# Fewer load buffers for the attention stage of an attention and mixture-of-experts kernel

## The chip, the cores and the metric

The kernel runs on one core of a Trainium2 chip. The metric is the device time of one execution in microseconds (us). The engines of the core are TensorE (PE), VectorE (DVE), ScalarE (ACT), GpSimd (POOL) and SyncE (SP); all loads and stores spoken of here are transfers that SP starts and that the core's 16 DMA engines carry out.

## What is computed

Attention over 4 batches and 8 heads, 768 tokens, head dimension 64, all in float32: each query sees the keys less than 16 tokens away and 24 summaries, one for each block of 32 tokens (the elementwise maximum of the block's keys, the mean of its values). Its output, laid out as tokens by 512, feeds a mixture of 8 experts with one expert per token, where a token may keep the expert of the token before it.

```python
k_sum = k.reshape(B, H, nb, block, D).max(axis=3)      # block 32, nb 24
v_sum = v.reshape(B, H, nb, block, D).mean(axis=3)
scores_l = scale * q @ k^T, masked to |i - j| < 16
scores_s = scale * q @ k_sum^T + log(block)
a = softmax(concat([scores_l, scores_s], axis=-1))
x = a @ concat([v, v_sum])                             # (B, S, H * D)
...
for s in range(S):                                     # for each batch b
    e = argmax(logits[b, s]) if s == 0 or local_gate[b, s] < 0.5 else prev_e
    out[b, s] = p[e] * (relu(x[b, s] @ w1[e]) @ w2[e])
```

## The kernel before

Attention works on 16 pairs of heads (4 batches of 4 pairs, `N = len(pairs)`), each pair `n` in two groups `G = 2n` and `2n + 1` of half the tokens. Four loads feed a pair: its keys into a `kp` buffer (`load_k`, 384 KB), its queries into `q` (`load_q`, 384 KB), its values into `vt` (`load_v`, 384 KB), and the values again, arranged as windows, into `vw` (`load_w`, 768 KB). K, Q, V and W below mean these four. Buffers are taken in turn, so pair `n` uses buffer `n % NK` and so on; a load into a buffer waits for the last reader of the pair that had it before.

The readers are these. Of `kp`: the block maxima on DVE (`reduce_k`, L245) and the copies into windowed keys `kb` on POOL (`windows`, L277), both one group or so before the pair's own scores. Of `q`: the score matmuls `s_mm` (L370) of both groups. Of `vt`: POOL's fold, DVE's sum and the gate matmuls (`gate_v`) in the pair's second group. Of `vw`: the output matmuls `a_mm` (L405), which come three groups after the scores (`LA = 3`); beside the loaded part of `vw`, POOL's `spread_v` (L307) and ACT's `gate_t` write the block means and gates into it. One group runs through `s_mm` on PE into `bs`, its maxima on DVE (`s_max`, L376, `nm`), the exponentials on ACT, transposes on PE, `a_mm` into `ba`, and the normalization on DVE into `xs`. Between these, the loop weaves in routing work for the tokens already done (L827, L858).

The order is written out by hand: `opening(G)` for the first six groups, then a loop over `G` in which each group's steps stand in a fixed order and `load_*` is called for a pair a few pairs ahead. Everything that SP does goes through it in program order, and an instruction that waits holds all that stand behind it. Beside the loads SP issues eight stores of finished attention output to DRAM (`x_dram`, 876 KB each, L567, two per batch, some groups after the batch's last pair), two constant loads at the end of `opening(4)`, one register load (`e_93`, L1380) and, when group 27 is through, the fetch of four weight chunks (`wst`, L1096, 512 KB each) of the first expert; four more follow after attention. An early DVE and POOL stretch clears the margins of the `kp`, `vt` and `vw` buffers once.

After attention (from about 118 us to the end) the experts' matmuls run; tokens are gathered from `x_dram` by POOL (L1118), transposed on PE (L1129), and the first weights are cast on ACT (`wcast`, L1373) into memory that the attention's buffers held before.

```python
NQ, NK, NV, NVW, NX = 5, 4, 4, 5, 4
```

Of the kernel before, what the change touches and what calls it, by code (L numbers as in the profile page):

```python
# [80 lines left out]

C_T, C_PE, C_WAIT, C_LONG, C_DVE, C_LAT, AHEAD = 0.65, 0.8, 0.3, 1.3, 0.14, 0.05, 1.5

NQ, NK, NV, NVW, NX = 5, 4, 4, 5, 4

LOCAL_THR = -1.4e-7

# [1 line left out]
class Kernel:  # L89
# [82 lines left out]
    def attention(self, tick, last):  # L172
        nc, tc, ident = self.nc, self.tc, self.ident
        with ExitStack() as ctx:
# [17 lines left out]
            def load_k(n):  # L192
                b, p = pairs[n]
                nc.sync.dma_start(out=kp[n % NK][:, 16:16 + S], in_=self.kT[b, p])

            def load_v(n):
                b, p = pairs[n]
                nc.sync.dma_start(out=vt[n % NV][:, 16:16 + S], in_=self.vT[b, p])

            def load_q(n):  # L200
                b, p = pairs[n]
                nc.sync.dma_start(out=qs[n % NQ], in_=self.qT[b, p])

            def load_w(n):
                b, p = pairs[n]
                nc.sync.dma_start(out=vw[n % NVW][:, AUX:NPL - AUX].rearrange("p j t c -> p (j t c)"), in_=self.vW[b, p][:, 0:P * NW])
# [36 lines left out]
            def reduce_k(n):  # L243
                ks = kss[n] = wk.tile([P, NB], F32, name="ks")
                nc.vector.tensor_reduce(out=ks, in_=by32(kp[n % NK][:, 16:16 + S]), op=ALU.max, axis=AX.X)  # L245
# [37 lines left out]
            def one_row(n):  # L283
                return groups[GATHER + 1][0] <= n
# [64 lines left out]
            def s_mm(G):  # L349

                n, g = groups[G]
                sp = live[G] = self.two_banks()
                quarters = [(h, c) for c in range(2) for h in range(2)]

                def at(h, c):
                    u = sp[64 * c:64 * c + 64, h, 0:NG * W].rearrange("p (u w) -> p u w", u=NG)
                    return slice(64 * h, 64 * h + 64), u

                for h, c in quarters:
                    r, o = at(h, c)
                    m0 = W * (2 * g + c)
                    nc.tensor.matmul(out=o.rearrange("p u w -> p (u w)"), lhsT=eye2[r], rhs=mask2[r, m0:m0 + NG * W],
                                     start=True, stop=False)
                for u in range(NG):
                    for h, c in quarters:
                        r, o = at(h, c)
                        t = 2 * (NG * g + u) + c
                        nc.tensor.matmul(out=o[:, u, :], lhsT=qs[n % NQ][r, 64 * t:64 * t + 64], rhs=kb[n % 2][r, t, :],  # L370
                                         start=False, stop=(u == NG - 1))

            def s_max(G):
                sp = live[G][:, :, 0:NG * W].rearrange("p h (u w) -> p h u w", u=NG)
                nm = wk.tile([P, 2, NG], F32, name="nm")
                nc.vector.tensor_reduce(out=nm, in_=sp, op=ALU.max, axis=AX.X, negate=True)  # L376
                live[G] = sp, nm
# [62 lines left out]
            def opening(G):  # L440

                s_mm(G)
                s_max(G)
                if G == 0:
                    s_exp(0)
                    reduce_k(1)
                    summaries(1)
                    gate_sums(True)
                    loads = (load_v, 2), (load_k, 3), (load_q, 3)
                elif G == 1:  # L450
                    gate_v(0)
                    s_exp(1)
                    reduce_v(0)
                    loads = (load_w, 2), (load_v, 3), (load_k, 4), (load_q, 4)
                elif G == 2:
                    sum_v(0)
                    spread_v(0)
                    s_exp(2)
                    gate_t(0)
                    t_stage(0)  # L460
                    loads = (load_v, 4), (load_w, 3)
                elif G == 3:
                    windows(2, nc.scalar, 0, NW // 2)
                    windows(2, nc.gpsimd, NW // 2, NW)
                    t_stage(1)
                    reduce_v(1)
                    reduce_k(2)
                    summaries(2, nc.vector)
                    gate_v(1)
                    s_exp(3)  # L470
                    a_mm(0)
                    a_norm(0)
                    loads = (load_k, 5), (load_q, 5)
                elif G == 4:
                    sum_v(1)
                    spread_v(1)
                    gate_t(1)
                    s_exp(4)
                    t_stage(2)
                    a_mm(1)  # L480
                    reduce_v(2)
                    reduce_k(3)
                    a_norm(1)
                    windows(3)
                    summaries(3)
                    loads = (load_v, 5), (load_w, 4)
                else:
                    keep = gate_v(2)
                    keep()
                    t_stage(3)  # L490
                    s_exp(5)
                    a_mm(2)
                    a_norm(2)
                    spread_v(2)
                    fold_v(3)
                    loads = (load_k, 6), (load_q, 6)
                for load, n in loads:
                    load(n)
                if G == 4:
                    for t, src in consts:  # L500
                        nc.sync.dma_start(out=t, in_=src)
# [9 lines left out]
            for G in range(OPEN, last_g + LA):  # L511
                tick(G, 6)
                if G == last_g:
                    ctx2.close()
                    self.split_weights()
                    self.free_banks()
                    self.clock()
                if G < last_g:
                    s_mm(G)
                n, g = divmod(G, GP)  # L520
                keep = gate_v(n) if g == 1 and n < len(pairs) else None
                if keep and one_row(n):
                    keep()
                if g == 0 and n <= len(pairs):
                    gate_t(n - 1)
                if LT <= G < last_g + LT:
                    t_stage(G - LT)
                if G < last_g:
                    s_max(G)
                    s_exp(G)  # L530
                    if G == OPEN:
                        reduce_v(3, folded.pop(3))
                    if keep and not one_row(n):
                        keep()
                    self.small(TIME[groups[G][1] if G < MORE else GP][0], True)
                tick(G, 0)
                if G < last_g:
                    self.small(TIME[groups[G][1] if G < MORE else GP][1], True)
                n, g = divmod(G, GP)
                if g == 1 and n < len(pairs) - 1:  # L540
                    reduce_v(n + 1, folded.pop(n + 1))
                if g == 0 and n < len(pairs) - 1:
                    reduce_k(n + 1)
                if LA <= G:
                    a_mm(G - LA)
                    a_norm(G - LA)
                if G < last_g:
                    n, g = groups[G]
                    N = len(pairs)
                    if g == 0:  # L550
                        if n + 1 < N:
                            windows(n + 1)
                            fold_v(n + 1)
                        if n + 2 < N:
                            if n + 3 < N:
                                load_v(n + 3)
                            load_w(n + 2)
                    else:
                        if n + 1 < N:
                            summaries(n + 1)  # L560
                        spread_v(n)
                        if n + 4 < N:
                            load_k(n + 4)
                            load_q(n + 4)
                while stores and stores[0][0] <= G:
                    _, t, x = stores.pop(0)
                    nc.sync.dma_start(out=self.x_dram[:, t:t + NG, :], in_=x.rearrange("p u a d -> p u (a d)"))  # L567
                tick(G, 5)
                tick(G, 1)
                if G < last_g:  # L570
                    self.small(TIME[groups[G][1] if G < MORE else GP][2], True)
                else:
                    self.flow(C_T)
# [1146 lines left out]
```

## Time and profile before

| | us |
|---|---|
| median of 3 runs (lowest, highest) | 414.23 (413.96, 414.83) |
| the profiled execution's own time | 417.37 |
| span of its trace | 415.6 |
| attention in it, to about | 118 |

The profiled execution is one more execution, with the profiler on; its own time stands 3.14 us above the median, and the span, from the first to the last instruction, 1.8 us below its own time. A row of a timeline is a run of like instructions: when the first started, the time to the end of the last, engine, line, operation, output and inputs with their shapes, how many, and in brackets how long the engine had stood idle before it and what ended that; "issue" there means that nothing in the profile was waited for. SPq is SP's queue of DMA issues: its rows tell when transfers were started, not when they landed. A window row tells how long each engine was busy in a stretch and with how many instructions.

### The profile page before, as it was taken

How to read it: one execution, taken by the hardware profiler on the slowest of the kernel's cores; microseconds unless marked ns; L12 is line 12 of the kernel's file. 1: busy time of each engine (PE TensorE's matmuls, PEld its weight loads, DVE VectorE, ACT ScalarE, POOL GpSimd, SP SyncE). 2: the span in 40 equal slices, each digit the busy share in tenths (PEclk: the TensorE clock that was granted, in tenths of full speed). 3: DMA queues.
4: the chain of work that ended last, by engine and by line, in shares of the span. 5: the costliest groups of instructions: out<-in, count | busy, mean ns of one | idle time of the engine just before them, and what ended most of it. 6: DMA issues, size and time to landing. Idle time of an engine off the chain costs nothing. (4 is left out here: it accounts for less than half of the span.)

```text
span 415.6 us, 10447 instructions
## 1 busy us (share of the span) xinstructions
PE 401.2 (97%) x3802; PEld 332.5 (80%) x3802; DVE 232.8 (56%) x516; ACT 186.9 (45%) x461; POOL 199.1 (48%) x334
## 2 busy tenths in 40 slices
PE   7999999999999999999999999999999999999993
PEld 6678777778798888888877877888998888889882
DVE  4778978989687777685232222263537433312631
ACT  4978877788874322156221002251535422101550
POOL 7599877877769300258503310063716460010552
PEclk9999999999999999999999999999999999999998
DMA  8999999999490200857777464128353670010011
GB/s 298 412 410 407 410 401 409 386 377 334 109 353 32 84 26 0 337 224 252 267 275 250 135 222 147 83 53 294 93 186 108 233 223 35 26 53 25 2 49 34
DMA packets 21936, 83.70 MB, mean 201 GB/s; under 512 B 2638, under 2 KB 3152, under 8 KB 18800
## 3 DMA queue, kind: packets, MB, share of 16 engines
q1 hardware_dynamic: 17600, 68.49, 44.2%
q0 software_dynamic: 4128, 14.22, 9.9%
q8 instruction: 32, 0.52, 0.5%
q10 hardware_dynamic: 144, 0.20, 0.2%
q14 instruction: 32, 0.26, 0.2%
HBM read 69.43 MB, written 13.60 MB: 200 GB/s over the span
## 5 line engine op out<-in xcount | busy, mean ns | idle before, releaser
L1253 ACT ACTIVATE hT<-bs 128x256 fp32r<-128x256 f32 (+1 forms) x88 | 34.6, 394 | 116.2 <-PE bs L1292 64.2
L1255 DVE SCALAR_TENSOR_TENSOR hT<-bs,hT 128x256 fp32r<-128x256 f32 (+1 forms) x88 | 38.3, 435 | 72.1 <-ACT hT L1253 72.0
L1147 PE MATMUL ba<-h,hT 128*128 128x512 f32 x192 | 77.9, 406 | 0.0
L1149 PE MATMUL ba<-h,hT 128*128 128x512 f32 x192 | 75.1, 391 | 0.0
L1148 PE MATMUL ba<-l,hT 128*128 128x512 f32 x192 | 74.9, 390 | 0.0
L1171 POOL DMA_INDIRECT out_dram<-yo,sidx x23 | 25.7, 1116 | 77.3 <-DVE yo L1163 36.7
L1290 PE MATMUL bs<-xT,h 128*128 128x512 f32 (+1 forms) x160 | 61.1, 382 | 0.0
L1291 PE MATMUL bs<-xT,h 128*128 128x512 f32 (+1 forms) x160 | 60.6, 379 | 0.0
L1292 PE MATMUL bs<-xT,l 128*128 128x512 f32 (+1 forms) x160 | 60.6, 379 | 0.0
L1118 POOL DMA_INDIRECT xg<-x_dram,gidx x26 | 30.0, 1154 | 62.6 <-PE ba L1149 27.5
L384 ACT ACTIVATE pr<-bs,nm 128x120 f32<-128x120 f32 x192 | 52.1, 382 | 4.8 <-DVE nm L376 4.5
L1109 POOL TENSOR_TENSOR l<-stg,h 128x256 fp32r<-128x256 f32 x48 | 37.6, 814 | 14.9 <-ACT h L1101 14.8
L1149 PEld LDWEIGHTS ba<-h,hT 128*128 128x128 f32 x192 | 36.0, 188 | 7.9
L1147 PEld LDWEIGHTS ba<-h,hT 128*128 128x128 f32 x192 | 36.1, 188 | 7.2 <-issue 0.8
L307 POOL COPY vw<-gs 24x432 f32<-24x432 f32 (+2 forms) x83 | 34.2, 431 | 15.5 <-issue 10.9
L1148 PEld LDWEIGHTS ba<-l,hT 128*128 128x128 f32 x192 | 36.2, 188 | 6.4
L1101 ACT CAST h<-stg 128x1024 fp32r<-128x1024 f32 x32 | 32.5, 1048 | 12.8 <-PE ba L1149 9.9
L1104 DVE TENSOR_TENSOR l<-stg,h 128x1024 fp32r<-128x1024 f32 x20 | 30.3, 1525 | 10.9 <-ACT h L1101 10.6
L1290 PEld LDWEIGHTS bs<-xT,h 128*128 128x128 f32 x160 | 30.0, 188 | 5.4 <-PE bs L1205 0.4
L1291 PEld LDWEIGHTS bs<-xT,h 128*128 128x128 f32 x160 | 30.0, 188 | 5.1 <-DVE xT L1124 0.2
L1292 PEld LDWEIGHTS bs<-xT,l 128*128 128x128 f32 x160 | 30.0, 188 | 5.0
L405 PE MATMUL ba<-vw,pt 121*64 121x76 f32 x768 | 32.5, 233 | 1.2 <-DMA vt<-in_vT 0.7
(271 smaller groups left out, 676.9 us busy)
## 6 DMA issues: line engine op xcount, KB each, us to landing
stg<-in_w SPq DMA_DIRECT2D x16, 1024.0 KB, 5.7
vw<-in_vW SPq DMA_DIRECT2D x16, 768.0 KB, 10.5
raw<-in_w SPq DMA_DIRECT2D x8, 1024.0 KB, 8.2
x_dram<-xs SPq DMA_DIRECT2D x8, 876.0 KB, 9.6
kp<-in_kT SPq DMA_DIRECT2D x16, 384.0 KB, 7.8
q<-in_qT SPq DMA_DIRECT2D x16, 384.0 KB
vt<-in_vT SPq DMA_DIRECT2D x16, 384.0 KB, 9.2
wst<-in_w SPq DMA_DIRECT2D x8, 512.0 KB, 9.2
```

Of the source, the lines that this page charges most:

```text
L307: nc.gpsimd.tensor_copy(out=bass.AP(dst.tensor, dst.offset, [dst.ap[0], (step, planes), (4, NW), (1, m)]), in_=bass.AP(src.tensor, src.off ...
L384: nc.scalar.activation(out=pr[:, h, u, :], in_=sp[:, h, u, :], func=AF.Exp, bias=nm[:, h, u:u + 1], scale=1.0)
L405: nc.tensor.matmul(out=ap[64 * c:64 * c + 64, u, h], lhsT=pt[0:W + 1, h, u, 64 * c:64 * c + 64], rhs=vw[n % NVW][0:W + 1, PL * h:PL * h + ...
L1109: eng.tensor_tensor(out=lo[:, p], in0=src[:, p], in1=hi[:, p].bitcast(F32), op=ALU.subtract)
L1147: nc.tensor.matmul(out=ps, lhsT=ah, rhs=wh, start=first, stop=False)
L1148: nc.tensor.matmul(out=ps, lhsT=ah, rhs=wl, start=False, stop=False)
L1149: nc.tensor.matmul(out=ps, lhsT=al, rhs=wh, start=False, stop=last)
L1253: self.nc.scalar.activation(out=h, in_=ps, func=AF.Relu)
L1255: self.nc.vector.scalar_tensor_tensor(out=l, in0=ps, scalar=0.0, in1=h.bitcast(F32), op0=ALU.max, op1=ALU.subtract)
L1290: nc.tensor.matmul(out=ps, lhsT=wh, rhs=xh[k], start=(k == 0), stop=False)
L1291: nc.tensor.matmul(out=ps, lhsT=wh, rhs=xl[k], start=False, stop=False)
L1292: nc.tensor.matmul(out=ps, lhsT=wl, rhs=xh[k], start=False, stop=(k == KT - 1))
```

## The change

The numbers of buffers go from 5 to 3 for queries, 4 to 2 for keys, 4 to 3 for values and 5 to 3 for value windows; the output buffers (`NX`) stay 4. The loads are asked for correspondingly later, as a buffer must be free: in the loop, the even group of pair `n` asks for W of pair `n + 1` (before: V of `n + 3`, then W of `n + 2`), and the odd group for K, Q and V of pair `n + 3` (before: K and Q of `n + 4`). The lists of `opening` follow suit. Nothing is changed in what is computed.

```diff
-NQ, NK, NV, NVW, NX = 5, 4, 4, 5, 4
+NQ, NK, NV, NVW, NX = 3, 2, 3, 3, 4
...
                 if G == 0:
-                    loads = (load_v, 2), (load_k, 3), (load_q, 3)
+                    loads = (load_v, 2), (load_k, 3)
                 elif G == 1:
-                    loads = (load_w, 2), (load_v, 3), (load_k, 4), (load_q, 4)
+                    loads = (load_q, 3), (load_w, 2), (load_v, 3)
                 elif G == 2:
-                    loads = (load_v, 4), (load_w, 3)
+                    loads = ()
                 elif G == 3:
-                    loads = (load_k, 5), (load_q, 5)
+                    loads = (load_k, 4), (load_q, 4), (load_v, 4)
                 elif G == 4:
-                    loads = (load_v, 5), (load_w, 4)
+                    loads = ((load_w, 3),)
                 else:
-                    loads = (load_k, 6), (load_q, 6)
+                    loads = (load_k, 5), (load_q, 5), (load_v, 5)
...
                         if n + 1 < N:
                             windows(n + 1)
                             fold_v(n + 1)
-                        if n + 2 < N:
-                            if n + 3 < N:
-                                load_v(n + 3)
-                            load_w(n + 2)
+                            load_w(n + 1)
                     else:
                         if n + 1 < N:
                             summaries(n + 1)
                         spread_v(n)
-                        if n + 4 < N:
-                            load_k(n + 4)
-                            load_q(n + 4)
+                        if n + 3 < N:
+                            load_k(n + 3)
+                            load_q(n + 3)
+                            load_v(n + 3)
```

On PE and ACT the instructions stand in the same order as before, but for the numbers of buffers; DVE has four and POOL six clearing instructions fewer at the start. What moves is SP's row. In the rows below, the name after DMA is the buffer with its number (`kp_125<-in_kT` loads keys), and the brackets name the semaphores waited for: DMAHW0 to DMAHW7 count finished transfers, each used by every eighth, and DVE, PE, Pool and Activation count that engine's work. The first place is the steady state on SP, from the keys of pair 12 on, in the kernel before:

```order
L194 DMA kp_125<-in_kT 128x768 [waits DMAHW6_49,DVE_49,Pool_49]
L202 DMA q_122<-in_qT 128x768 [waits DMAHW7_49]
L198 DMA vt_131<-in_vT 128x768 [waits DMAHW0_49,PE_49,Pool_49]
L206 DMA vw_136<-in_vW 128x1536 [waits DMAHW1_49,Activation_49]
L194 DMA kp_126<-in_kT 128x768 [waits DMAHW2_49,DVE_49,Pool_49]
L202 DMA q_123<-in_qT 128x768 [waits DMAHW3_49]
L567 DMA x_dram<-xs_142 128x3x584 [waits DMAHW4_49,DVE_49]
```

The same place on SP in the changed kernel, from the keys of pair 12 up to the second store of the batch:

```order
L194 DMA kp_123<-in_kT 128x768 [waits DMAHW6_49,DVE_49,Pool_49]
L202 DMA q_120<-in_qT 128x768 [waits DMAHW7_49,PE_49]
L198 DMA vt_127<-in_vT 128x768 [waits DMAHW0_49,PE_49]
L565 DMA x_dram<-xs_135 128x3x584 [waits DMAHW1_49]
L206 DMA vw_132<-in_vW 128x1536 [waits DMAHW2_49,PE_49,Activation_49]
L565 DMA x_dram<-xs_136 128x3x584 [waits DMAHW3_49,DVE_49]
```

Q and W now wait for PE too, and the keys and queries of pair 13, which stood ahead of the batch's first store, come after its second (the register load of L1378 stands between). The W in both is that of pair 11. The second place is the end of attention on SP, the last rows of loads, the weights and the third batch's stores, in the kernel before:

```order
L206 DMA vw_139<-in_vW 128x1536 [waits DMAHW7_49,Activation_49]
L206 DMA vw_135<-in_vW 128x1536 [waits PE_49,DMAHW0_49,Activation_49,Pool_49]
L1096 ISA
L1096 DMA wst_2230<-in_w 128x1024 [waits DMAHW1_49]
...
L1096 DMA wst_2236<-in_w 128x1024 [waits DMAHW4_49]
L567 DMA x_dram<-xs_140 128x3x584 [waits DMAHW5_49,DVE_49]
L567 DMA x_dram<-xs_141 128x3x584 [waits DMAHW6_49,DVE_49]
```

The same on SP in the changed kernel:

```order
L206 DMA vw_132<-in_vW 128x1536 [waits DMAHW7_49,PE_49,Activation_49]
L1094 ISA
L1094 DMA wst_2212<-in_w 128x1024 [waits DMAHW0_49]
...
L1094 DMA wst_2218<-in_w 128x1024 [waits DMAHW3_49]
L206 DMA vw_130<-in_vW 128x1536 [waits PE_49,DMAHW4_49,Activation_49,Pool_49]
L565 DMA x_dram<-xs_133 128x3x584 [waits DMAHW5_49,DVE_49]
L565 DMA x_dram<-xs_134 128x3x584 [waits DMAHW6_49,DVE_49]
```

The W of the last pair, which stood ahead of the four weight fetches, now stands behind them and just ahead of the two stores.

## Rows read from the trace of the kernel before

**Rows 1.** Page, busy us of each engine, share of the span, instructions:

```profile
PE 401.2 (97%) x3802; PEld 332.5 (80%) x3802; DVE 232.8 (56%) x516; ACT 186.9 (45%) x461; POOL 199.1 (48%) x334
```

**Rows 2.** Page: packets, MB, share of a queue; issues, KB each, median us to landing:

```profile
q8 instruction: 32, 0.52, 0.5%
...
vw<-in_vW SPq DMA_DIRECT2D x16, 768.0 KB, 10.5
...
x_dram<-xs SPq DMA_DIRECT2D x8, 876.0 KB, 9.6
```

**Rows 3.** Timeline of SP's issues: start us, us, line, output and input, count:

```profile
77.87 0.33 SPq L194 DMA_DIRECT2D kp<-in_kT  x1
...
83.29 5.04 SPq L206 DMA_DIRECT2D vw<-in_vW  x2
88.54 2.36 SPq L1096 DMA_DIRECT2D wst<-in_w  x4
93.55 3.89 SPq L567 DMA_DIRECT2D x_dram<-xs  x2
```

**Rows 4.** Timeline of PE, 48 to 108 us, output matmuls and "issue" stops:

```profile
51.82 1.01 PE L405 MATMUL ba<-vw,pt 121*64 121x76 f32 x24
...
68.26 0.42 PE L370 MATMUL bs<-kb,q 64*64 64x120 f32 x4 [0.93 <-issue]
...
74.89 0.57 PE L370 MATMUL bs<-kb,q 64*64 64x120 f32 x10 [0.20 <-issue]
...
79.77 1.01 PE L405 MATMUL ba<-vw,pt 121*64 121x76 f32 x24
81.62 0.64 PE L370 MATMUL bs<-kb,q 64*64 64x120 f32 x15 [0.27 <-issue]
...
88.80 0.83 PE L370 MATMUL bs<-kb,q 64*64 64x120 f32 x21 [0.48 <-issue]
...
100.72 1.01 PE L405 MATMUL ba<-vw,pt 121*64 121x76 f32 x24
```

**Rows 5.** Timeline of DVE, 60 to 92 us, the instructions after idle time:

```profile
68.73 0.91 DVE L376 TENSOR_REDUCE nm<-bs 128x6 f32<-128x720 f32 x1 [0.66 <-PE bs L370]
69.90 0.23 DVE L332 COPY gs<-bt 64x73 f32<-64x73 f32 x1 [0.26 <-ACT gs L329]
75.49 0.91 DVE L376 TENSOR_REDUCE nm<-bs 128x6 f32<-128x720 f32 x1 [0.16 <-PE bs L370]
76.67 0.23 DVE L332 COPY gs<-bt 64x73 f32<-64x73 f32 x1 [0.27 <-ACT gs L329]
```

**Rows 6.** Windows: us; busy (count) PE, PEld, DVE, ACT, POOL; clock, DMA share, GB/s:

```profile
48.49:54.79 6.30, 5.99 (x126) 4.76 (x126) 5.15 (x10) 4.80 (x17) 5.37 (x12) 1.00 1.03 401
68.23:74.87 6.64, 6.43 (x125) 5.12 (x126) 5.71 (x16) 5.25 (x18) 4.81 (x12) 1.00 1.03 404
81.60:88.78 7.18, 6.50 (x125) 5.14 (x126) 7.00 (x16) 5.32 (x18) 6.52 (x15) 1.00 1.02 410
88.78:107.25 18.47, 18.25 (x377) 15.03 (x378) 17.18 (x46) 15.81 (x52) 14.01 (x32) 1.00 0.76 275
```

**Rows 7.** DMA queue q8, packets in 72.3 to 73.6, then 107.2 to 107.5:

```profile
q8 instruction: 1, 0.02, 5.2%
...
q8 instruction: 1, 0.02, 19.3%
```

**Rows 8.** Timeline of POOL: key windows of pairs 6, 8; block means of 8, 15:

```profile
38.43 1.46 POOL L277 TENSOR_SCALAR kb<-kp 128x384 f32<-128x384 f32 x3
51.12 1.46 POOL L277 TENSOR_SCALAR kb<-kp 128x384 f32<-128x384 f32 x3
62.99 2.60 POOL L307 COPY vw<-gs 24x432 f32<-24x432 f32 x6 [1.29 <-issue]
...
111.47 2.33 POOL L307 COPY vw<-gs 24x432 f32<-24x432 f32 x5 [1.59 <-ACT gs L332]
```

**Rows 9.** Timeline of ACT and PE after the last group's scores:

```profile
114.55 1.07 ACT L1373 CAST h<-wst 128x1024 fp32r<-128x1024 f32 x1
114.65 0.66 PE L1129 MATMUL bs<-ident,xg 128*128 128x128 f32 x4
```

## The prediction

> **What bounds the kernel now.** First the busy times of the engines: TensorE (PE) works through 97% of the span, so only the few per cent in which it stands still can come back [rows 1]. Next, what is queued for the DMA engines: a window-value load takes 10.5 us from issue to landing (median), an attention-output store 9.6 [rows 2], although the windows show the queues at a share of 1.02 to 1.03 and 401 to 410 GB/s [rows 6], at which 768 KB need 1.9 us (768 KiB = 0.79 MB over 404 GB/s). The loads are not slow; they stand behind other loads, asked for up to four pairs ahead. Up to about 65 us SP, the engine that issues them, is paced by the eight transfers that may be outstanding (each of its rows waits for the one eight places back, DMAHW0 to 7). After that the loads of the last pairs go out as their buffers come free: the queue is empty at 77.87 and refilled at once [rows 3].
>
> Then TensorE's timeline. Inside four score stages it stands still with nothing that the profile shows to wait for ("issue"): 0.93 us before 68.26, 0.20 before 74.89, 0.27 before 81.62, 0.48 before 88.80 [rows 4]. From one such stop to the next the windows count 125 matmuls with 126 weight loads, then 377 with 378 over three such lengths [rows 6]: about 251 records each time, a few records being missing from a trace and some uncounted instructions lying between. The instruction queue q8 moves 32 packets of 16 KB in the run (0.52 MB) [rows 2]. I read these as blocks of TensorE's instructions, and each stop as a block that came late.
>
> The decisive view is where those packets fall. After the stop at 68.26 no q8 packet runs from 68.3 to 72.3; the next lies in 72.3 to 73.6, and the stop before 74.89 follows. After 107.25, with the data queue empty, a q8 packet runs within 0.3 us [rows 7], and no "issue" stop follows. So the fetch of the next block appears to start when TensorE crosses into a block, and to wait until most of the data queued at that moment has gone. A stop ends some 2.3 us after the start of its packet (72.3 to 73.6, against 74.89). A block occupies TensorE for about 6.0 us (5.99 in 48.49 to 54.79 [rows 6]); a start up to 6.0 − 2.3 = 3.7 us late therefore costs nothing, a later one what is over.
>
> The Trainium skill, "Runtime: NRT & Kernel Launch", section "Instruction fetch mechanics", says that instructions come in 16 KiB blocks of 256 through a DMA queue of the sequencer's own, and that crossing into a block is mostly hidden. The packet size and the record counts agree; "hidden" does not while the data queue is full, as the 0.93 us show. By that sentence the sum below would be zero.
>
> **The change part by part.**
>
> *Buffers and memsets.* K loses two buffers (four DVE memsets), V one (two POOL), W two (four POOL). They stand before the first loads land and the first score stage waits for keys, not for them. Zero; without that cover at most ten times some 0.2 us on POOL, a gain.
>
> *Waits.* In the steady state SP issues K, Q, V of a pair and W of the next one in turn, each now after the last reader of the third pair back (K: second back): K after DVE's block maxima and POOL's windows, Q and V after TensorE's scores and gates, W after the second group's output matmuls. Behind a waiting load everything later on SP waits: loads, stores and at the end the weights. Are they still early enough? The keys of pair 8 may go after POOL's windows of pair 6 at 38.43 + 1.46 = 39.89 and are read from 51.12: 11.2 us. Pair 8's W may go after the output matmuls at 51.82 + 1.01 = 52.83; the POOL copy that writes beside it starts at 62.99: 10.2 us [rows 4, 8]. Ahead of such a W stand at worst K, Q and V (3 × 384 KB) and one 876 KB store: 1.18 + 0.90 MB, 5.1 us at 404 GB/s; with its own 1.9 us it is through after 7.0, and I allow 1 us more for its way there and back. Margin 2 us, so no wait on compute is added: zero. Cover gone means that each us of delay lengthens a pair, of which about twelve are in the steady state.
>
> *Queue depth.* Here the gain lies. With loads asked for 1.5 to 2 pairs ahead, what stands in front of TensorE's block fetch is one pair's group: the 1.9 us of a W, or 2.9 us of K, Q and V, in place of up to eight transfers. That is below 3.7 us, so the stops at 68.26, 74.89 and 88.80 vanish. The block fetched after the W of pair 12 (issued at 79.77 + 1.01 = 80.78 [rows 4]) is an example: of that W 0.79 − 0.33 = 0.46 MB are left at the boundary 81.60. Where two output stores fall among the loads (the block that ends at 81.60, and the two near 42 and 48.5) 4.6 to 6.7 us remain queued by the same addition, so I leave the stop at 81.62 in, and those of 48 to 55 us too.
>
> What that is worth depends on VectorE (DVE), which is nearly as full there: 7.00 of 7.18 us in 81.60 to 88.78 and 17.18 of 18.47 after it [rows 6]. Only DVE idle time that the late block caused is won: 0.66 + 0.26 around 68.73, and 0.16 + 0.27 around 75.49 [rows 5]. The stop at 88.80 is counted at zero because DVE stays full behind it. Sum: 0.92 + 0.43 = **1.35 us**. Bounds: DVE swallows it all, 0; or TensorE gets back every stop, 0.93 + 0.20 + 0.27 + 0.48 = 1.88, with some 0.6 for two like stops near 48.5 and 54.8, 2.5.
>
> *End of attention.* SP's row there becomes: last-but-one W, four 512 KB weight fetches, last W, two stores. Before, the last W left ahead of the weights (88.0 us, inside the group from 83.29), the weights from 88.54, the stores from 93.55 [rows 3]. Now the last W waits for output matmuls that end at 100.72 + 1.01 = 101.73 [rows 4]; the POOL copy that needs it runs from 111.47 [rows 8]. Ahead of it stand the W before it, released one pair earlier at about 95, and the weights (2.10 MB, 5.2 us): through at about 102. It lands at about 102 + 1.9 + 1 to 3 = 105 to 107: over 4 us early. The two stores follow it: 1.79 MB, 4.4 us, about 109 to 111, against ScalarE's cast from 114.55, which waits for their buffers; the gathers that share the queue with them are first read at 114.65 [rows 9]. Zero; cover 3 us.
>
> *Early part.* The first twenty rows of SP keep their order, and a constant load moves ahead of pair 5: zero. Of the run's 415.6 us, everything after about 118 us is untouched.
>
> So the profiled execution, 417.37 us, becomes 416.0. It lies 3.14 us above the median of the runs, 414.23; the same 1.35 us off that gives **412.9**.
>
> **The rivals.**
>
> *No change, 414.2.* The waiting fetch might get a fixed share of the DMA engines whatever stands behind, or the stops go and DVE makes TensorE wait in their place. For it: DVE's 7.00 of 7.18 us; at 81.60 the packet is late too and DVE alone would fill the gap. Against it: the start of a packet moves from over 4 us to 0.3 with the queue's depth [rows 7]. Time 414.2, give or take 0.5.
>
> The Trainium skill, "DMA: Bandwidth & Descriptors", section "Queues, rings and completion order", says that each DMA engine turns from ring to ring after every packet. By that rule a fetch should not wait for depth at all, and this rival would hold; the 4 us without a q8 packet under a full queue speak against it.
>
> *Slower: the last W comes late.* If from issue it takes not 4 but the 10.5 us that such loads took before [rows 2], it lands at 101.8 + 10.5 = 112.3, 0.8 us after POOL wants it at 111.47; it decides from 9.7 us. The two stores behind it go to 116.7, 2.2 us past the cast of 114.55. That is +1 to +2 and without the gain 415.2 to 416.2. For it: SP's row is strictly in order and the W waits for TensorE now. Against: the 10.5 is a deep queue's, which the change itself removes.
>
> *It doesn't do what it says.* If the eight outstanding transfers still paced SP, the queue would stay as full and nothing would move: 414.2, part of the first rival. This holds up to about 40 us, where the loads have no buffer to wait for; not after it, where W leaves no earlier than its matmuls.
>
> **How the numbers follow.** A measurement of this kernel can tell about 0.2%, 0.83 us, from no change. Forecast (gain of 0.83 to 2.5, 411.7 to 413.4): 0.47. No change with the last rival: 0.35. Slower, 415.1 and up: 0.18. The gain's own range is 411.8 to 413.4; 8 in 10 takes in no change and reaches the nearer end of the slower case, 411.8 to 415.2, which leaves out about 0.15 above and 0.03 below.
>
> **What would show it.** Right: in the changed profile no "issue" stop of over 0.1 us before the score matmuls near 68, 75 and 88 us, q8 packets within 3 us of each block's start, the median time of W loads down from 10.5 to 4 to 7 us, DVE's idle before its maxima there gone. Wrong: the stops stay though the queue is shorter; DVE or POOL wait for a DMA in the middle of attention; the POOL copy of the last pair or the cast after it wait for a DMA; or the start of the weights, 114.55 us, has not moved.

## The result and the profile after

The changed kernel is slower: 418.24 us in the median of 4 runs (416.39 to 421.27) against 414.28, a ratio of the mean times of 1.0102 (95% interval 1.0055 to 1.0148). A second measurement of the same kernel, 12 runs, gave 416.93 us against 414.80 and 1.0055 (1.0025 to 1.0084). Forecast were 412.9 us and a range of 411.8 to 415.2. The changed kernel's runs also spread wider: over 5.7 us in those 12, against 3.6 in 35 of the kernel before beside them.

The first lines are from the page after: the engines' busy times, the granted clock in 40 slices (9 is full), and two DMA issues with KB and median us to landing.

```profile
PE 401.5 (96%) x3802; PEld 333.8 (80%) x3802; DVE 232.9 (56%) x512; ACT 187.3 (45%) x461; POOL 198.7 (48%) x328
...
PEclk9999989999999999999999999999999999999998
...
vw<-in_vW SPq DMA_DIRECT2D x16, 768.0 KB, 6.3
x_dram<-xs SPq DMA_DIRECT2D x8, 876.0 KB, 9.1
```

The W loads land after 6.3 us instead of 10.5 [rows 2], as forecast, and TensorE has the same work. But one slice of the clock row, the sixth (52 to 62 us), is not full, and TensorE's timeline shows why. Its "issue" stops of over 0.4 us after, one stretch of output matmuls before and one behind the longest stop, and the first transpose of gathered tokens; then, of the kernel before, the stop that stands in the place of the longest:

```profile
42.87 0.89 PE L405 MATMUL ba<-vw,pt 121*64 121x76 f32 x21 [0.75 <-issue]
...
45.70 1.01 PE L405 MATMUL ba<-vw,pt 121*64 121x76 f32 x24
...
50.55 0.33 PE L394 MATMUL bt<-ident,pr 128*120 128x128 f32 x1 [1.63 <-issue]
...
50.92 1.67 PE L405 MATMUL ba<-vw,pt 121*64 121x76 f32 x24
...
77.07 0.57 PE L370 MATMUL bs<-kb,q 64*64 64x120 f32 x10 [0.47 <-issue]
90.88 0.84 PE L370 MATMUL bs<-kb,q 64*64 64x120 f32 x21 [0.48 <-issue]
116.06 0.66 PE L1127 MATMUL bs<-ident,xg 128*128 128x128 f32 x4 [0.35 <-DMA xg<-x_dram,gidx]
```

```profile
48.50 0.33 PE L394 MATMUL bt<-ident,pr 128*120 128x128 f32 x1 [0.32 <-issue]
```

The stop before 68.26 and the one before 81.62 [rows 4] are gone, but 0.75 us before 42.87 and 1.63 us before 50.55 are new, where the kernel before lost 0.32 at 48.50. After the longer one, 24 output matmuls take 1.67 us in place of 1.01. The windows (busy us and counts of PE, PEld, DVE, ACT, POOL; granted clock, DMA share, GB/s) give the clock:

```profile
42.87:48.09 5.22, 5.22 (x122) 4.37 (x121) 4.69 (x11) 3.90 (x14) 4.99 (x12) 1.00 0.98 311
44.00:46.00 2.00, 2.00 (x45) 1.67 (x38) 1.97 (x5) 0.86 (x4) 1.81 (x6) 1.00 0.97 244
51.00:52.00 1.00, 1.00 (x20) 1.00 (x21) 0.85 (x2) 1.00 (x4) 0.81 (x4) 0.54 0.93 357
52.00:53.00 1.00, 1.00 (x18) 0.78 (x18) 0.34 (x2) 0.97 (x4) 1.00 (x3) 0.50 1.02 389
53.00:54.00 1.00, 1.00 (x28) 0.85 (x20) 0.47 (x1) 0.00 (x0) 1.00 (x3) 0.50 1.05 402
54.00:55.00 1.00, 1.00 (x14) 0.83 (x7) 0.69 (x1) 0.13 (x1) 0.44 (x1) 0.75 1.09 417
```

TensorE stood still for 1.63 us and then had the lower of its two levels (1.2 GHz) for about 3.4 us, which costs 0.46 + 0.50 + 0.50 + 0.25 = 1.7 us of full-speed work. Matmul by matmul, the trace after falls behind the trace before by 3.6 us from 42 to 55 us; 1.9 are left at 73 us, where the old stop at 68.26 is missing, and 2.1 when the last group starts. At the experts' first matmul 1.4 are left (119.65 against 118.24 us), in a second trace of the changed kernel (below) 0.3 (118.50). The execution traced before stands 3.1 us above its kernel's median, so the traces tell where time is lost inside attention, not how much the medians differ.

Why the block that TensorE wanted at 48.9 came at 50.5 is seen on SP's issues after, and in the DMA queues of 48.0 to 48.3 us:

```profile
39.60 0.33 SPq L206 DMA_DIRECT2D vw<-in_vW  x1
40.03 0.37 SPq L194 DMA_DIRECT2D kp<-in_kT  x1
40.50 0.38 SPq L202 DMA_DIRECT2D q<-in_qT  x1
41.00 0.86 SPq L198 DMA_DIRECT2D vt<-in_vT  x1
41.91 0.44 SPq L565 DMA_DIRECT2D x_dram<-xs  x1
46.78 0.34 SPq L206 DMA_DIRECT2D vw<-in_vW  x1
47.22 0.42 SPq L565 DMA_DIRECT2D x_dram<-xs  x1
```

```profile
q8 instruction: 1, 0.02, 19.1%
```

W, K, Q, V and a store leave within 2.8 us, because the W, held by the output matmuls, held all of them; 4.9 us after the store the next W goes, when the output matmuls of 45.70 have ended (45.70 + 1.01 = 46.71). Up to 118 us, W loads on SP wait for output matmuls 13 times after, 46.5 us in all, and once, for 4.2 us, before. TensorE entered a block at 42.87, and no q8 packet runs until the one above, 5.2 us later. The same wait for all blocks of both kernels, worked out from the traces (a block's entry is the start of its first matmul, found by its place in TensorE's order; us to the start of the next q8 packet / GB/s of the other packets that start meanwhile; blocks entered near 36, 42, 48, 55, 61, 68, 75 and 82 us in the kernel before):

```
before             3.8/414  3.8/415  3.8/413  3.7/404  4.7/415  4.1/408  4.2/384  4.8/404
after              4.8/337  5.2/306  4.4/387  3.5/344  3.9/305  4.6/282  4.1/415  5.0/405
after, second run  3.6/363  4.9/300  3.7/410  3.7/420  3.8/338  5.1/272  4.8/411  4.4/407
stores together    4.2/360  3.4/341  5.0/314  3.8/412  5.2/406  2.2/407  0.5/12   2.5/387
four W buffers     3.5/407  3.4/338  4.7/401  3.7/414  3.5/275  6.0/305  3.8/326  2.3/400
deep, new order    3.7/412  4.1/398  3.8/396  3.9/402  4.6/416  4.2/403  1.7/100  4.0/339
```

(The last three are experiments below.) Two things are read here. Before, the wait is 3.7 to 4.8 us, and it does not follow the depth of the queue (the bytes of loads and stores that SP has issued, less those whose packets have started): of 3.6 MB queued at 48.50 only 1.6 were moved before the packet started (3.8 us); at 74.89 only 1.8 MB were queued, 1.6 were moved, and it took 4.2. The change did make the queue shallower, from 1.8 to 3.6 MB at these eight entries to 0.8 to 2.6, but the waits are 4.1 us in the mean before and 4.4 after. And after, the waits of 4.6 us and more at 36, 42 and 68 go with 282 to 337 GB/s; the one of 5.0 at 82 does not (405).

### The profile page after: what moved, and what is told of

Same layout as the page of the kernel before. It is cut to its first block, busy times and chain, and to the rows that moved or that the text cites. A ratio compares the mean times of both kernels' runs of the same rounds, so it can differ in the third digit from the quotient of the medians.

```text
span 416.4 us, 10450 instructions
## 1 busy us (share of the span) xinstructions
PE 401.5 (96%) x3802; PEld 333.8 (80%) x3802; DVE 232.9 (56%) x512; ACT 187.3 (45%) x461; POOL 198.7 (48%) x328
## 5 line engine op out<-in xcount | busy, mean ns | idle before, releaser
L1102 DVE TENSOR_TENSOR l<-stg,h 128x1024 fp32r<-128x1024 f32 x20 | 30.9, 1555 | 10.8 <-ACT h L1099 10.5
L405 PE MATMUL ba<-vw,pt 121*64 121x76 f32 x768 | 33.6, 236 | 2.0 <-issue 1.1
L405 PEld LDWEIGHTS ba<-vw,pt 121*64 121x64 f32 x768 | 28.4, 139 | 7.8 <-issue 6.0
```

What stands on the lines that cost most here:

```text
L405: nc.tensor.matmul(out=ap[64 * c:64 * c + 64, u, h], lhsT=pt[0:W + 1, h, u, 64 * c:64 * c + 64], rhs=vw[n % NVW][0:W + 1, PL * h:PL * h + ...
```

## The experiments

Theory A: TensorE's blocks come late behind the transfers that a held SP releases in a burst. B: the loss is in late loads, above all the last W and the stores behind it. C: two K buffers are too few. Times are medians of 4 to 12 runs, ratios are against the kernel before on the same chip.

**Which buffers.** Five W buffers again and W asked for as before:

```diff
-NQ, NK, NV, NVW, NX = 3, 2, 3, 3, 4
+NQ, NK, NV, NVW, NX = 3, 2, 3, 5, 4
...
-                            load_w(n + 1)
+                        if n + 2 < N:
+                            load_w(n + 2)
```

> The changed kernel with five W buffers again and W asked for two pairs ahead as before; K, Q and V stay at 2, 3 and 3 buffers. Theory A (loads are released in a burst of K, Q, V and W together, and TensorE's instruction block fetch waits behind the burst): K, Q and V still hold SP back, the W goes out right behind them, so the burst is as large; stops like those of the changed kernel (0.75 and 1.63 us near 42.9 and 50.6), 416 to 419 us. Theory B (the single W arrives late, above all the last one with the two stores behind it): as the kernel before, about 414 us.

Measured 414.12 us, 0.9985 (0.9958 to 1.0012). The counterpart is the kernel before with W alone made shallow:

```diff
-NQ, NK, NV, NVW, NX = 5, 4, 4, 5, 4
+NQ, NK, NV, NVW, NX = 5, 4, 4, 3, 4
...
-                            load_w(n + 2)
+                            load_w(n + 1)
```

> The kernel before with only W made shallow (three buffers, asked for one pair ahead); K, Q, V as before. Theory A: W now holds SP back until the output matmuls end, and K, Q, V and W go out in one burst a pair, with the stops of the changed kernel, 416 to 419 us. Theory B: the late W is all there is to the loss, also 416 to 419 us. A rival C, that two K buffers are too few: about 414 us.

Measured 418.62 us, 1.0078 (1.0047 to 1.0108). With W deep, shallow K, Q and V cost nothing that can be measured; W alone made shallow loses as the whole change does. C falls, and so does A's first form, by which the first of the two should have lost as well: in its trace SP releases K, Q, V, a store, W and a second store from 39.80 to 42.88 us and then nothing to 46.74, so a burst by itself is not the loss. TensorE's longest stops, first with W alone shallow, then with W deep:

```profile
68.36 0.42 PE L370 MATMUL bs<-kb,q 64*64 64x120 f32 x4 [1.33 <-issue]
...
76.64 0.57 PE L370 MATMUL bs<-kb,q 64*64 64x120 f32 x10 [1.85 <-issue]
```

```profile
74.72 0.57 PE L370 MATMUL bs<-kb,q 64*64 64x120 f32 x10 [0.78 <-issue]
```

**The wait or the order.** With `NVW` 4 in the changed kernel SP's rows stand in the same order, and only the W's wait for the output matmuls goes:

> The changed kernel with a fourth W buffer and nothing else: SP's rows stand in the same order, but the W loads wait no longer for TensorE's output matmuls of the pair that ended last. Theory A, now sharper (the block fetch waits for about 1.5 MB of whatever is queued, 3.7 to 4.3 us; it takes 5 to 6 us where SP is held by a W that waits and a store is left alone at the tail of the queue): the W follows the store at once, no stop over 0.8 us, 414 to 415 us. Theory B (the order at the end of attention, the last W behind the weights, is the loss): 416 to 418.5 us, as the order has not changed.

Measured 415.30 us, 1.0015 (0.9990 to 1.0041). This points at the wait and not at the order, though the interval overlaps that of the changed kernel (1.0025 to 1.0084). Its trace still has one bad place. TensorE enters a block at 66.72, SP issues K, Q, V, a store, W and a store from 66.84 to 69.63 us and then, as its register load waits for DVE, nothing to 78.2; the wait for the block is 6.0 us, and the clock is at its lower level behind the stop:

```profile
66.84 0.33 SPq L194 DMA_DIRECT2D kp<-in_kT  x1
...
69.23 0.40 SPq L565 DMA_DIRECT2D x_dram<-xs  x1
78.23 0.33 SPq L194 DMA_DIRECT2D kp<-in_kT  x1
```

```profile
75.14 0.57 PE L370 MATMUL bs<-kb,q 64*64 64x120 f32 x10 [2.13 <-issue]
```

```profile
77.00:78.00 1.00, 1.00 (x7) 0.66 (x7) 0.89 (x6) 0.48 (x2) 0.61 (x2) 0.50 1.06 395
```

Here the queue was nearly empty at the entry, 0.4 MB, and 3.8 MB were issued behind it; so what SP issues after a block is entered delays its fetch as well. The block entered at 60.76, with 0.2 MB queued and K, Q, V and W issued from 60.79 on, waits 3.5 us.

The register load was then moved to just ahead of the weights, still with four W buffers:

```diff
-            st["e0"] = nc.values_load(self.e0[0:1, 0:1], engines=(ENG.SP,), min_val=0, max_val=E - 1)
+            def e0_load():
+                st["e0"] = nc.values_load(self.e0[0:1, 0:1], engines=(ENG.SP,), min_val=0, max_val=E - 1)
+            at(WFETCH - 1, 1, e0_load)
```

> The changed kernel with a fourth W buffer and SP's register load, which holds SP right behind the second store of batch 1 until about 77 us, moved to just ahead of the weight fetches. Theory A: no store is left alone any more, the stop of 2.1 us near 75 seen with the fourth buffer alone goes, 413 to 414.5 us and no drop of the clock near 76. Otherwise 415 us as with the fourth buffer alone.

Measured 416.56 us, 1.0049 (1.0028 to 1.0070), with a stop of 1.85 us at 75.56. A hold right behind a store is therefore not what makes the block late there. And this kernel, in whose trace no W waits for output matmuls, loses about as much as the changed one: the wait of W is one way to the loss, not the only one.

**The stores.** In the changed kernel, the first store of batches 0 and 1 one group later:

```diff
-stores.append((G + LA + (2, 2, 3, 0)[b], t, x))
+stores.append((G + LA + (3 - g, 3 - g, 3, 0)[b], t, x))
```

> The changed kernel with the first store of batches 0 and 1 one group later, so that both stores of a batch stand behind the waiting W with K, Q and V right behind them. Theory A: no store is left alone in the queue, the stop of 1.63 us near 50 falls below 0.9 us, the clock stays at full speed in the middle of attention, 415 to 416.5 us. Theory B: 418 us, since W and the end are as they were.

Measured 415.60 us, 1.0017 (0.9995 to 1.0039). SP's row then reads:

```profile
46.23 0.33 SPq L206 DMA_DIRECT2D vw<-in_vW  x1
46.60 0.96 SPq L565 DMA_DIRECT2D x_dram<-xs  x2
47.67 1.35 SPq L194 DMA_DIRECT2D kp<-in_kT  x1
```

By the medians most of the loss is gone with no buffer added; the interval still overlaps that of the changed kernel. Its trace is not free of stops, one of 1.13 us at 55.50 and this one:

```profile
69.51 0.42 PE L370 MATMUL bs<-kb,q 64*64 64x120 f32 x4 [1.49 <-issue]
```

That a lone store is the slow one was tested by cutting each of these stores into three, one group after another:

> The changed kernel with each 876 KB store of batches 0 and 1 cut into three of 292 KB, asked for one group after another. Theory A (an instruction block waits for some 1.5 to 2 MB to be moved, and an 876 KB store that runs alone behind a held SP moves at about 250 to 300 GB/s): no lone store lasts long, the waits for blocks between 42 and 80 us stay below 5 us, no stop over 1 us, 414 to 415.5 us. Theory E (it is the bursts of loads, not the stores, that make a block late): 416.5 to 418.5 us as the changed kernel.

Measured 416.99 us, 1.0038 (1.0015 to 1.0061), and its trace has the old stop in the old place:

```profile
50.35 0.32 PE L394 MATMUL bt<-ident,pr 128*120 128x128 f32 x1 [1.63 <-issue]
```

The lone store falls, and the packets of the changed kernel say so too: from 44.0 to 46.5 us, at 220 to 270 GB/s, all large packets are of 3,072 bytes, which are K, Q and V loads; the store's 2,336-byte ones begin at 46.95. Mean us of one such packet, over half microseconds in which nothing else large moves, 8 to 95 us:

```
before            0.123 (0.121 to 0.127)
after             0.141; 0.16 to 0.27 in 44.0 to 46.5, 0.15 to 0.28 in 73.5 to 76.5
after, second run 0.143; up to 0.28 in 43.5 to 45.5, up to 0.29 in 70.5 to 72.5
stores together   0.124 (0.121 to 0.139)
```

The loads themselves are at times half as fast where SP works in bursts, and not in the kernel before with its fuller queue. What slows them was not found. Nor are slow loads by themselves the loss: the mean goes up to 0.42 us in the trace with W deep, and to 0.30 and 0.27 in those of the half and the quarter shift below, and none of the three kernels is slower than before.

**Where the blocks begin.** TensorE's warm-up was changed to 24 full and 84 tiny matmuls, which with their weight loads are 128 instructions more, in the changed kernel and in the kernel before:

```diff
-WARM = 44
+WARM, TINY = 24, 84
...
+            for _ in range(TINY):
+                nc.tensor.matmul(out=wb[0:32, 0:1], lhsT=self.wz[:, 0:32], rhs=self.wz[:, 0:1], start=True, stop=True)
```

> The changed kernel with 128 more instructions in TensorE's warm-up (24 full and 84 tiny matmuls in place of 44 full ones), which moves every 256-instruction block boundary by half a block, some 3 us, and leaves loads and buffers alone. Theory A: the boundaries no longer fall just behind a burst near 42.9 and 48; the stops of 0.75 and 1.63 us go, the granted clock stays at full speed there, 414 to 416 us. Theories B and C: 418 us as the changed kernel.

> The kernel before with the same half block shift. Theory A: its stops move to other places; with a queue that is always full they stay of like size, 413 to 415.5 us. Theories B and C: 414.2 us, no change.

Measured 414.90 us, 1.0009 (0.9984 to 1.0034), and 414.62 us, 1.0000 (0.9976 to 1.0023). The same loads at other block boundaries lose nothing that can be measured. The edit is not a pure shift, as it also thins the warm-up: in the first of these traces the granted clock is 0.50 from 7.1 to 10.4 us, in the first scores, where the changed kernel's is full, so the gain is not from there. With 64 instructions more (34 and 42), beside the changed kernel once more, unedited:

> The changed kernel with a quarter block of shift (34 full and 42 tiny warm-up matmuls, 64 instructions more), loads as they are. Theory A: time depends on where the boundaries fall; boundaries 1.5 us earlier than in the changed kernel still lie in front of the lone store, 415 to 418 us, between the changed kernel and the half-block shift. Theory D (the loss is in the loads themselves and the half-block shift helped by chance): 418 us.

> The changed kernel once more, unedited, for its spread and a second trace. Theory A (a store left alone behind a W that waits makes the next instruction block late; how late hangs on where the block boundary falls): slower than before by 0.6 to 1.2%, 416.5 to 419 us, with at least one stop of 1 us or more in attention and runs that spread over some 4 us. If the first measurement was chance: 414 to 415 us.

Measured 414.83 us, 0.9971 (0.9949 to 0.9993), and 416.93, 1.0055 (1.0025 to 1.0084). The second trace of the changed kernel has these stops:

```profile
48.92 0.32 PE L394 MATMUL bt<-ident,pr 128*120 128x128 f32 x1 [1.34 <-issue]
...
75.06 0.57 PE L370 MATMUL bs<-kb,q 64*64 64x120 f32 x10 [1.05 <-issue]
...
114.90 0.66 PE L1127 MATMUL bs<-ident,xg 128*128 128x128 f32 x4 [1.07 <-DMA xg<-x_dram,gidx]
```

The first two stand at the same instructions as 50.55 and 77.07 in the first trace; their sizes differ, the stop of 0.75 us is missing, and the clock stays full. A control for the quarter shift has the changed kernel's order of loads with the buffers of before (5, 4, 4, 5), called the deep kernel from here on:

> The changed kernel's order of loads with the buffers of before (5, 4, 4, 5) and the quarter block shift (34 full and 42 tiny warm-up matmuls): a control for the quarter shift of the changed kernel and a candidate for the best. If the shift itself is worth the 0.3% that it gave there, 412.5 to 413.5 us; if it only moved the boundaries of the changed kernel away from the lone stores, 414 to 415 us.

Measured 418.71 us, 1.0098 (1.0077 to 1.0120). The shift is not good in itself; here it puts stops where the unshifted deep kernel has none:

```profile
35.69 0.42 PE L372 MATMUL bs<-kb,q 64*64 64x120 f32 x4 [1.57 <-issue]
...
57.14 0.84 PE L372 MATMUL bs<-kb,q 64*64 64x120 f32 x22 [1.15 <-issue]
...
109.08 0.63 PE L372 MATMUL bs<-kb,q 64*64 64x120 f32 x14 [1.16 <-issue]
```

**The end of attention.** First the four weight fetches one group later (`WFETCH` 28), behind the last W and one store:

> The changed kernel with the four weight fetches one group later, so that the last W and the first store of the third batch stand ahead of them. Theory A: the stops near 42.9 and 50.6 stay, 417 to 418.5 us. Theory B: the end is mended, 414 to 415.5 us.

Measured 424.15 us, 1.0217 (1.0178 to 1.0256). The old stops stay (1.76 us at 49.91), so this mended nothing; the late fetches pushed a store back behind them, and ScalarE's first cast waited for it, then TensorE for ScalarE. Waits of 95 to 125 us (us in total, times, longest) and TensorE's row:

```profile
ACT h L1371 <- DMA x_dram<-xs: 6.1, 1, 6.1
```

```profile
122.44 1.35 PE L405 MATMUL ba<-vw,pt 121*64 121x76 f32 x24 [3.89 <-ACT pt L395]
```

Behind that stop the granted clock is 0.50 to 130 us, for 6.8 us, which costs another 3.4 us of full-speed work; so this run says little on the place of the last W.

Then the last W alone. In the changed kernel it got a buffer of its own:

```diff
+def VI(n):
+    return 3 if n == 15 else n % NVW
```

> The changed kernel with a buffer of its own for the last pair's W (a fourth one, used by pair 15 alone), so that this load, behind the weights as before, waits for no matmul, and the two stores behind it go out earlier; all else as changed. Theory B, now for the end alone (the last W holds back the stores of batch 2, these the gathers, and TensorE waits for them): no wait on a gather near 115, and from the last group's first matmul to the first routing transpose 17.25 us in place of 17.5 to 19.5; about 1.5 us less than the changed kernel, 415 to 416.5. Theory A alone: 417 to 418.5 us.

and in the deep kernel with the new order it was made to wait as in the changed one (`2 if n == 15`):

> The changed kernel's order of loads with the deep buffers of before, but the last pair's W put into the buffer of pair 12, so that it alone waits for the same matmuls as in the changed kernel. Theory B for the end: the gather wait of 0.35 to 1.4 us and the stretch of 17.5 to 19.5 us come back, 415 to 416.5 us, 1.5 us over the same kernel without it. Theory A alone: about 414 to 414.5 us as without it.

Measured 418.03 us, 1.0052 (1.0031 to 1.0073), and 415.75 us, 0.9991 (0.9970 to 1.0012), against 0.9971 (0.9954 to 0.9988) for the deep kernel without it, on the same chip. Neither trace waits for a gather. All eight traces taken before these two with three W buffers do, 0.35 to 1.38 us near 115 (the row at 116.06 above is one), but taking the late W away gave nothing that can be measured. Adding it cost some 0.2%, with intervals that overlap, and did not bring the gather wait back, so it does not price that wait. Both remedies together, its own last buffer and the stores together:

> The changed kernel with the last pair's W in a buffer of its own and the two stores of batches 0 and 1 together behind the waiting W: both suspected costs taken away at 3, 2, 3 and 3 + 1 buffers. If A and B together are the loss: 413.5 to 415 us, no gather wait near 115. If something else of the shallow loads costs time: 415.5 to 417.

Measured 416.36 us, 1.0019 (0.9994 to 1.0044), no better than the stores alone (1.0017), whose result it repeats. So B is at best a small part.

**The order with deep buffers**, to tell order from buffers and as a candidate, measured twice:

> The changed kernel's order of loads with the kernel before's numbers of buffers (5, 4, 4, 5). Theory A: waits go, the queue is full as before, about 414 to 415 us. Theory B: the order at the end is kept, 415.5 to 418 us.

> The changed kernel's order of loads with the buffers of before (5, 4, 4, 5) once more, the best so far beside the quarter shift: 0.9979 with an interval that reaches 1.0004. If the order is worth something: 413 to 414 us and again below 1; if not, 414 to 415 us.

Measured 413.92 us, 0.9979 (0.9954 to 1.0004), and 414.69 us, 0.9971 (0.9954 to 0.9988): this one beats both kernels, by a quarter of a per cent. Where from? In its order SP's register load stands ahead of pair 13's loads, and the queue is all but empty when TensorE enters the block at 74.5 (1.7 us to the next packet, at 100 GB/s, in the table above). The stops at 81.62 and 88.80 [rows 4] do not occur in its trace; the last one in attention is

```profile
74.49 0.57 PE L370 MATMUL bs<-kb,q 64*64 64x120 f32 x10 [0.21 <-issue]
```

With the register load moved out of that place:

> The order of loads of the changed kernel with the deep buffers of before (5, 4, 4, 5) and the register load moved likewise: meant as the best of both. Theory A: the queue stays full through 70 to 78 us, the stops keep 0.2 to 0.9 us, 413 to 414.5 us.

Measured 415.52 us, 1.0013 (0.9993 to 1.0034), and the two stops are back:

```profile
80.99 0.64 PE L370 MATMUL bs<-kb,q 64*64 64x120 f32 x15 [0.28 <-issue]
...
88.17 0.84 PE L370 MATMUL bs<-kb,q 64*64 64x120 f32 x21 [0.48 <-issue]
```

They are 0.76 us together, while the two ratios stand some 1.7 us apart, and the trace with the stops even reaches the experts earlier (116.58 against 117.15 us). That the gain is these two stops is therefore not shown.

## Why the prediction was wrong

**What bounds the kernel** held: stops in the middle of a stage are late instruction blocks. In every trace the stops at block entries end 2.2 to 2.7 us after a q8 packet's start, and moving the boundaries moves them.

**The step that failed** is the one that says a fetch waits "until most of the data queued at that moment has gone". It was drawn from two ends, over 4 us behind a full queue and 0.3 behind an empty one [rows 7], as if the wait grew with depth between them, so that a shallower queue would bring the blocks in time. The queue did get shallower (0.8 to 2.6 MB at the entries in place of 1.8 to 3.6) and the waits did not get shorter (4.4 us in the mean, 4.2 in the second trace, before 4.1). The rows of before already spoke against it: 3.8 us with 3.6 MB queued, 4.2 us with 1.8. In the sixteen traces without a shift, with eight such entries each, 29 entries had 2.9 MB or more queued and waited 3.5 to 4.4 us, whatever the depth. With less queued the waits go from 0.5 to 6.0 us, and what is issued behind the entry counts: 6.0 us with 0.4 MB queued and 3.8 issued meanwhile (four W buffers, 66.72), 1.7 us with 0.2 queued and nothing issued (the deep kernel with the new order, 74.49). Nor was the queue "empty at 77.87", as the prediction read from SP's rows: 0.6 MB were left, and 381 GB/s moved from 77.5 to 78.0 us.

The Trainium skill's rule in "DMA: Bandwidth & Descriptors" ("Queues, rings and completion order"), that each engine turns from ring to ring, agrees with the traces so far as the wait does not grow with depth from 2.9 MB on; it does not explain the 3.5 us and more that remain.

**Queue depth, second error.** What stands in front of a fetch was put at "the 1.9 us of a W, or 2.9 us of K, Q and V". They come together: SP is in order, so the wait that holds W holds K, Q, V and a store as well, and 1.97 MB (2.86 with a store) are released within 1.8 to 3.6 us in the two traces of the changed kernel. The part on waits had named this queueing behind the waiting load, and drew only its effect on when loads arrive, not on what the fetch finds.

**The stops left in** "near 42 and 48.5" were held to be as before. In one trace the one near 42, which is not there before, came to 0.75 us; the one at 48.5 grew from 0.32 to 1.63 us, in the other trace to 1.34. The fetches behind the two long ones had begun 5.2 and 4.9 us after the entry, at 306 and 300 GB/s, and once the clock fell, for another 1.7 us. That term was put at zero.

**The loads' margins** were right: no engine waits for a load in the middle of attention after. **The sum** of 1.35 us on VectorE lost its ground with the stops: the one at 68.26 did vanish, that at 88.80 stayed at 0.48, and 0.47 stood at 77.07 in place of the 0.20 before 74.89.

**The end of attention**, put at zero with 3 us of cover, was wrong in most traces by the gather wait of 0.35 to 1.38 us; its share of the time is too small to measure. **The slower rival** had the right sign and the wrong place: not the last W's landing, but the waits of the W loads all through attention; the loss by the medians, 4.0 and 2.1 us, is above its 1 to 2. The Trainium skill, "Runtime: NRT & Kernel Launch", section "Instruction fetch mechanics", calls the crossing into a block mostly hidden; stops of up to 2.13 us say otherwise here.

**What stays open:** what sets the 3.5 us and more that a fetch waits; why K, Q and V packets take at times over twice as long where SP issues in bursts; why putting two stores together takes most of the loss away, with stops of 1.13 and 1.49 us left; why the kernel with four W buffers loses again once the register load is moved; and how much of the loss is the clock, which fell within attention in five traces behind "issue" stops of 1.13 to 2.13 us, but in others with 1.63 and 1.76 did not. That W's buffers and the place of the block boundaries decide is shown by runs; how the late fetches add up to the medians is argued from one or two traces each.

## What to carry to other kernels

Before shortening buffers, find the wait that then binds on the queue's issuing engine and list everything behind it: in order, one late buffer turns a steady stream into bursts. A fourth W buffer, which removed one wait, came out level with the kernel before (1.0015) with K, Q and V still shallow, but at 1.0049 with one register load moved. Where a kernel runs thousands of small instructions beside a full DMA queue, look for "issue" stops a fixed count apart, and measure a change at two or three shifts of the instruction stream before believing half a per cent.

## What was not expected of the hardware

A shift of TensorE's instructions by 64, a quarter of a block, made in the warm-up with the loads left alone, moved the time from 1.0055 to 0.9971 in the changed kernel and from 0.9971 to 1.0098 in the deep one with the same order: as much as any edit of buffers here. A block's fetch waits 3.5 to 4.4 us behind a queue of 2.9 MB or more, whatever its depth, and up to 6.0 us behind shallower ones to which SP adds in bursts. And after a standstill of 1.63 us TensorE ran for 3.4 us at 0.50 of its clock, which doubled the price of that stop.
